# First MLP pass fed from SBUF instead of DRAM, in a three-stage transformer kernel

## The chip, the cores and the metric

The kernel runs on one NeuronCore of a Trainium2 chip. The metric is device time in microseconds (us) from one launch; three runs of the kernel before the change took 1973.47, 1975.07 and 1977.85 us, so its median is 1975.07 us.

## The reference

The inputs are q, k, v of 8 batches, 8 heads, 576 positions and 64 columns, and weights; all is float32. Cut to what matters:

```
# 1. landmark attention per batch and head (32 landmarks = means over 18 positions)
A, Bm, C = softmax(q @ k_lm.T), softmax(q_lm @ k_lm.T), softmax(q_lm @ k.T)   # scale 1/8
Z = Bm.T / (norm_1(Bm) * norm_inf(Bm) + 1e-6); six times: Z = 2Z - Z @ Bm @ Z
x = concat_heads(A @ Z @ C @ v)                      # (8, 576, 512)
# 2. token mixing of rank 32, then an MLP
u = x + ((x.T @ U) @ V).T
x = u + relu(u @ w_ch1) @ w_ch2                      # 512 -> 2048 -> 512
# 3. Fourier mixing, norm, a second MLP
u = x + real(fft(fft(x, axis=1), axis=2))
un = (u - mean(u)) / sqrt(var(u) + 1e-6)
out = u + relu(un @ moe2_w_ch1) @ moe2_w_ch2
```

## The kernel before

Activations are kept transposed: 512 features in four blocks of 128 partitions, positions along the row. The 8 x 576 positions are cut into nine **chunks** of 512 columns, so that chunk c begins 64c columns into batch c and ends in the next batch. Each float32 matmul of the MLPs is made of three products of rounded halves (high, low), for which x, g and the weights are split: ScalarE casts the high half, VectorE or GpSimd subtracts to get the low one (`split`, lines 51 and 52).

Each MLP is done in two **passes** of half its hidden layer, four passes in all (`Mlp.stream`). A pass goes through the nine chunks; a chunk takes 16 **steps**: in eight up steps (m = 0 to 7) it makes `up(m)` = 12 matmuls of 128x512 (lines 213 to 215), ScalarE's relu (217) and VectorE's low half (218); in eight down steps, two for each output block d, 24 matmuls a block (lines 258 to 260), the addition of a residual (267) and the write `dst.put`. The first pass takes its residual from the x tiles and writes y1; the second takes x anew and y1 as residual and writes x1, from which the Fourier stage (`Mixer`, one per batch, 24 steps apart, first at step 33 of the second pass) loads U at its first step (line 689) and folds it four steps later (698). Passes three and four do the second MLP.

The order of the work is written out by hand: `Slots` hold closures by step, and each engine and each DMA queue executes its instructions in the order of the program. Nearly all DMAs are issued from SyncE's queue, those of u1 from ScalarE's.

Attention of one batch (`Batch.steps`) spans relative steps 0 to 25: landmarks 0 to 3, the kernel matrix and its inverse 5 to 19 (`newton` 14 to 19), scores 6 to 11, `values` 12, `query` 12 to 14, its norm 14 and 15, `heads` 20, `rank` 21, `mix(i)` 22 to 25. `mix` multiplies out block i of u1 (with token mixing folded in), copies it from PSUM to the tile u1T, and ScalarE's queue writes that to `u1[b]` in DRAM. Blocks 2 and 3 go to rows shifted by one, since the Fourier stage wants features 257 to 511 in reverse order behind 256: block 2 to rows 257 to 384, block 3 to rows 385 to 511 (127 partitions) and, as a one-row write, row 256. Batch 0 begins at step -32, batch b at 16(b - 2); the first pass begins at step 0. In the steps ahead of that TensorE also does six small filler matmuls a step (line 935). x of chunk 0 is loaded from u1 at step -6 and split from there on; x of a later chunk is loaded in the chunk before it, at d = 1, and split from d = 2.

The weights come as float64 and are converted on chip (`convert`: per weight tile of 128x512 four yields, with four VectorE operations at lines 96, 97, 100, 103 and one at 106, one GpSimd addition at 104, ScalarE's abs at 101, then a split). For the first pass `direct` does that while attention runs: 87 yields in all with the set-up of U and V, drawn by `some(convs, n)`, n a step. Raw tiles 0 to 13 use the buffers of g, the others two of their own. Weights of later passes are converted and staged to DRAM (`staging`), and fetched into the eight w1 and eight w2 tiles.

Of the kernel before, what the change touches and what calls it, by code (L numbers as in the profile page):

```python
# [9 lines left out]
F32 = mybir.dt.float32  # L10
# [13 lines left out]
P = 128  # L24
# [15 lines left out]
def body(ctx: ExitStack, tc: tile.TileContext, qT, kT, vn, mU, mV, w11, w12, w21, w22,  # L40
# [91 lines left out]
    class ByBatch:  # L132
# [9 lines left out]
        def put(self, c, d, sb):  # L142
            for cc, b, cb in pieces(c):
                nc.sync.dma_start(self.tiles[b][rows(d), cb], sb[:, cc])

    class ByChunk:
        def __init__(self, tiles):
# [16 lines left out]
    class Mlp:  # L164
# [4 lines left out]
        def __init__(self, pool, ps, banks, passes):  # L169
            self.pool, self.ps, self.banks, self.passes = pool, ps, banks, passes  # L170
            self.w1, self.w2 = [], []
            self.n = 0

# [26 lines left out]

        def start(self):
            self.nx = []
            self.xf = self.load(0, self.passes[0][0])
            self.more = self.split_x(self.xf, nc.vector)

# [16 lines left out]
        def stream(self, p, tail=None):  # L222
            x_src, res_src, dst, _ = self.passes[p]
            for c in range(NCH):
                x, self.nx = self.nx, []
                last = c + 1 == NCH
                res = self.xf if res_src == "x" else self.tiles() if res_src is None else None
                after = (p, c + 1) if not last else (p + 1, 0) if p + 1 < len(self.passes) else None
                g = []
                for m in range(HM):  # L230
                    g.append(self.up(m, x))
                    if m == 1 and res is None:
                        res = self.load(c, res_src)
                        if tail:
                            sc = self.tail_pool.tile([P, NC], F32, name="sc", bufs=2)
                            tail[0].get(c, sc)
                            skip = [self.tail_pool.tile([P, NC], F32, name="skip", bufs=8) for _ in range(4)]
                            for d in range(4):
                                tail[1].get(c, d, skip[d])
                    if m == 3 and after and p:  # L240
                        self.xf = self.load(after[1], self.passes[after[0]][0])
                    yield 1
                if last:
                    self.w1 = self.w1[HM:]
                    if after:
                        for m in range(HM):
                            self.fetch("w1", self.passes[p + 1][3][m])
                more, w2 = iter(()), self.w2[:HM]
                for d in range(4):
                    if d == 1 and after and p == 0:  # L250
                        self.xf = self.load(after[1], self.passes[after[0]][0])
                    if d == (0 if p else 2) and after:
                        more = self.split_x(self.xf)
                    ps = self.bank()
                    for k in range(HM):
                        gh, gl = g[k][:, 0, :], g[k][:, 1, :]
                        wh, wl = w2[k][:, 0, rows(d)], w2[k][:, 1, rows(d)]
                        nc.tensor.matmul(ps, wh, gh, start=k == 0, stop=False)  # L258
                        nc.tensor.matmul(ps, wl, gh, start=False, stop=False)  # L259
                        nc.tensor.matmul(ps, wh, gl, start=False, stop=k == HM - 1)  # L260
                        if k == HM // 2 - 1:
                            next(more, 0)
                            yield 1
                    if res_src is None:
                        nc.scalar.copy(res[d], ps)
                    else:
                        nc.vector.tensor_tensor(res[d], ps, res[d], op=ALU.add)  # L267
                    if tail:
                        nc.vector.tensor_tensor(res[d], res[d], sc, op=ALU.mult)
                        nc.vector.tensor_tensor(res[d], res[d], skip[d], op=ALU.add)  # L270
                    dst.put(c, d, res[d])
                    next(more, 0)
                    yield 1
                if last:
                    self.w2 = self.w2[HM:]
                    if after:
                        for k in range(HM):
                            self.fetch("w2", self.passes[p + 1][3][HM + k])

# [10 lines left out]
    def attention_constants(cp, t):  # L290
# [8 lines left out]
        t["at"] = cp.tile([P, 4, S], F32, name="at")  # L299
        t["Bf"] = cp.tile([P, 2, P], F32, name="Bf")  # L300
        t["W"] = cp.tile([P, 4, P], F32, name="W")
        nc.gpsimd.memset(t["Bf"], 0.0)
        nc.gpsimd.memset(t["W"], 0.0)
# [23 lines left out]
    class Batch:  # L327
# [7 lines left out]

        def __init__(self, pool, psb, t, b):
            self.pool, self.psb, self.t, self.b = pool, psb, t, b
            self.E, self.ET, self.ps = {}, {}, {}
# [31 lines left out]
        def kernel(self):  # L370

            t, qb, kb = self.t, self.t["qb"], self.t["kb"]
            ps = self.bank("b")
            for g in range(2):
                for e in range(2):
# [14 lines left out]
            for e in range(2):  # L390
                sl = self.EJ[e]
                nc.vector.tensor_tensor(t["Bf"][sl, :, sl], sB[sl], r[sl].unsqueeze(2).to_broadcast([64, 2, 64]),
                                        op=ALU.mult)
            nc.vector.tensor_tensor(self.sums[:, :, 0], s, r, op=ALU.mult)

        def kernel_t(self):
            ps = self.bank("b")
            for g in range(2):
                nc.tensor.transpose(ps[:, g * P:g * P + P], self.t["Bf"][:, g, :], ident_sb)
            v = ps[:, 0:2 * P].rearrange("p (g c) -> p g c", g=2)  # L400
# [178 lines left out]
        def heads(self):  # L579
# [3 lines left out]
            for g in range(2):  # L583
                nc.tensor.matmul(ps[:, 64 * g:64 * g + 64], self.t["Bf"][:, g, :], self.ry[:, g, P:192], start=True,
                                 stop=True)
# [21 lines left out]
        def mix(self, i):  # L607
            W_, at, u = self.t["W"], self.t["at"], u1[self.b]
            u1T = self.pool.tile([P, S], F32, name="u1T", bufs=2)
            pss = []  # L610
# [5 lines left out]
            nc.scalar.copy(u1T[:, HS:S], pss[1][:, 0:HS])  # L616
            if i < 2:
                nc.scalar.dma_start(u[i * P:(i + 1) * P, :], u1T)
            elif i == 2:
                nc.scalar.dma_start(u[257:385, :], u1T)  # L620
            else:
                nc.scalar.dma_start(u[385:512, :], u1T[0:127])
                nc.scalar.dma_start(u[256:257, :], u1T[127:128])

        def steps(self, after):
# [10 lines left out]
            yield from ((14 + i, lambda i=i: self.newton(i)) for i in range(6))  # L636
            yield from ((20, self.heads), (21, self.rank))
            yield from ((22 + i, lambda i=i: self.mix(i)) for i in range(4))
            if after:
# [221 lines left out]
    class Slots:  # L861
# [9 lines left out]
        def run(self, s):  # L871
            for step in self.at.pop(s, ()):
# [6 lines left out]
            [w21[i] for i in range(HM, NM)] + [w22[i] for i in range(HM, NM)]]  # L879
    U1, X1, U2, UN, Y = ByBatch(u1), ByBatch(x1), ByBatch(u2), ByBatch(un), ByBatch([out[b] for b in range(B)])  # L880
    passes = [(U1, "x", ByChunk(y1), None), (U1, ByChunk(y1), X1, staged[1]),
              (UN, None, ByChunk(y2), staged[2]), (UN, ByChunk(y2), Y, staged[3])]
# [5 lines left out]
    with pool("mm") as mp, pool("pm", space=PSUM) as pm:  # L888
        mlp = Mlp(mp, pm, 3, passes)

        def direct():
# [20 lines left out]
            for i in range(len(ws)):  # L912
                fetch()
                new = convert(cv0, raws[i], ws[i], 2)
# [5 lines left out]

        EARLY = 14
        with pool("aa") as ap_, pool("ac") as ac, pool("cv0") as cv0, pool("pt", space=PSUM) as psb:
            t = {}
            batches = [Batch(ap_, psb, t, b) for b in range(B)]
            slots = Slots()
            FIRST = -32
            X0 = FIRST + Batch.LAST + 1
            for b in range(B):
                slots.add(FIRST if b == 0 else STEPS * (b - 2), batches[b].steps(batches[b + 1] if b + 1 < B else None))

# [6 lines left out]
            with tc.manual_schedule():  # L937
# [6 lines left out]
                for s in range(FIRST, 0):  # L944
                    slots.run(s)
                    if s > FIRST + 5:
                        filler()
                    if s == X0:
                        mlp.start()
                    elif X0 + 2 < s:  # L950
                        some(mlp.more, 2)
                    some(convs, 0 if s < FIRST + 4 else 3 if s < FIRST + 10 or s > X0 else 2)
                later, gen = staging(cv0, 1, 2), mlp.stream(0)
                for s in range(N):
                    next(gen)
                    slots.run(s)
                    if s < HM:
                        some(convs, 3)
                        if s == HM - 1:
                            some(convs, 99)  # L960
                    else:
                        some(later, 2 if s % 4 == 0 else 1)
                some(later, 999)
# [102 lines left out]
```

## Time and profile before

| | |
|---|---|
| median of three runs | 1975.07 us |
| span of the profiled execution | 1966.8 us |
| TensorE busy | 1898.4 us, 97% |
| VectorE busy | 939.6 us, 48% |
| ScalarE busy | 558.1 us, 28% |
| GpSimd busy | 366.8 us, 19% |
| DMA, read and written | 132 GB/s over the span |

Busy time counts an engine's instructions, from the first to the last of the program. The span is that of one execution taken by the hardware profiler; the profile gives its span and not a time with the launch. In the page and the views, PE is TensorE, DVE is VectorE, ACT is ScalarE, POOL is GpSimd and SP is SyncE, whose rows are DMA issues; a q behind an engine's name marks its sequencer. L213 is line 213 of the kernel.

### The profile page before, as it was taken

To read this page: it belongs to the slowest core of one execution; us is meant where nothing else is said; L and a number is where in the kernel's file an instruction comes from. 1 tells how busy PE (TensorE), PEld (TensorE's weight loads), DVE (VectorE), ACT (ScalarE), POOL (GpSimd) and SP (SyncE) were. 2 spreads that over 40 slices of the span, in tenths; PEclk is the share of its full clock that TensorE was granted. 3 is DMA by queue.
4 is the path that set the end of the run, shared out by engine and by line. 5 is a ranking of instruction groups with operands and counts; after the bars stand their busy time and mean duration, and the time that the engine had idled before them with its cause. 6 is when DMAs were issued, how large, how long until landed. Compare 5 with 4: busy or idle time off the path is not lost.

```text
span 1966.8 us, 27786 instructions
## 1 busy us (share of the span) xinstructions
PE 1898.4 (97%) x11096; PEld 1562.5 (79%) x11096; DVE 939.6 (48%) x1628; ACT 558.1 (28%) x1153; POOL 366.8 (19%) x346
## 2 busy tenths in 40 slices
PE   6778999999999999999999999999999999999998
PEld 5666777777778888888888888888888888888887
DVE  6785465555433244474574454654532133333333
ACT  2433333333322222233232333433322211111110
POOL 2441011111111122131331122313211000010000
PEclk9999999999999999999999999999999999999999
DMA  7234335343324643354453562433422453323332
GB/s 251 92 107 130 119 107 177 102 139 126 110 88 145 228 153 131 127 166 160 133 162 105 210 225 81 164 125 120 140 91 91 149 203 122 99 91 97 97 97 75
DMA packets 145874, 262.35 MB, mean 133 GB/s; under 512 B 22768, under 2 KB 77904, under 8 KB 145744
## 3 DMA queue, kind: packets, MB, share of 16 engines
q1 hardware_dynamic: 141248, 251.14, 38.2%
q10 hardware_dynamic: 4496, 9.44, 1.3%
q8 instruction: 87, 1.43, 0.3%
q14 instruction: 43, 0.35, 0.1%
HBM read 166.93 MB, written 93.59 MB: 132 GB/s over the span
## 4 chain that ended last, share of the span: by engine, by line
PE 80%; DVE 8%; DMA 6%; ACT 2%; issue 2%; ACTq 0%; POOL 0%; SPq 0%; DVEq 0%; POOLq 0%
PE ps L213 12%; PE ps L215 12%; PE ps L214 12%; PE ps L258 11%; PE ps L260 11%; PE ps L259 11%; DMA u<-u1T 5%; PE ps_f L76 1%; PE ps_f L77 1%; PE ps_f L78 1%; PE ps_n L613 1%; PE ps_n L572 1%; DVE g L218 1%; DMA xf<-u 1%; DVE cva L106 1%
## 5 line engine op out<-in xcount | busy, mean ns | idle before, releaser
L213 PE MATMUL ps<-x,w 128*128 128x512 f32 x1152 | 460.2, 399 | 1.7 <-ACT x L51 1.7
L258 PE MATMUL ps<-g,w 128*128 128x512 f32 x1152 | 458.4, 398 | 0.0
L215 PE MATMUL ps<-x,w 128*128 128x512 f32 x1152 | 450.1, 391 | 0.9 <-POOL x L52 0.9
L260 PE MATMUL ps<-g,w 128*128 128x512 f32 x1152 | 449.7, 390 | 0.0
L214 PE MATMUL ps<-x,w 128*128 128x512 f32 x1152 | 449.2, 390 | 0.0
L259 PE MATMUL ps<-g,w 128*128 128x512 f32 x1152 | 448.8, 390 | 0.0
L218 DVE SCALAR_TENSOR_TENSOR g<-ps,g 128x512 fp32r<-128x512 f32 x288 | 198.5, 690 | 459.9 <-ACT g L217 459.4
L217 ACT ACTIVATE g<-ps 128x512 fp32r<-128x512 f32 x288 | 171.9, 597 | 644.8 <-PE ps L215 644.3
L213 PEld LDWEIGHTS ps<-x,w 128*128 128x128 f32 x1152 | 216.7, 188 | 48.1 <-issue 2.8
L215 PEld LDWEIGHTS ps<-x,w 128*128 128x128 f32 x1152 | 216.3, 188 | 48.1 <-POOL x L52 1.4
L260 PEld LDWEIGHTS ps<-g,w 128*128 128x128 f32 x1152 | 216.2, 188 | 46.4
L258 PEld LDWEIGHTS ps<-g,w 128*128 128x128 f32 x1152 | 216.3, 188 | 46.2 <-issue 2.6
L259 PEld LDWEIGHTS ps<-g,w 128*128 128x128 f32 x1152 | 216.6, 188 | 43.0
L214 PEld LDWEIGHTS ps<-x,w 128*128 128x128 f32 x1152 | 216.8, 188 | 42.7
L267 DVE TENSOR_TENSOR xf<-ps,xf 128x512 f32<-128x512 f32 x108 | 74.4, 689 | 259.7 <-PE ps L260 232.1
L104 POOL TENSOR_TENSOR cvp<-cvp,cva 128x512 f32<-128x512 f32 x64 | 86.0, 1344 | 536.2 <-DVE cvp L103 536.1
L52 POOL TENSOR_TENSOR x<-xf,x 128x512 fp32r<-128x512 f32 x70 | 94.0, 1349 | 473.2 <-ACT x L51 445.1
L51 ACT CAST x<-xf 128x512 fp32r<-128x512 f32 x144 | 85.3, 618 | 60.4 <-DMA xf<-u 60.1
L52 POOL TENSOR_TENSOR stg<-cva,stg 128x512 fp32r<-128x512 f32 x48 | 68.7, 1431 | 133.7 <-ACT stg L51 133.7
L52 DVE TENSOR_TENSOR x<-xf,x 128x512 fp32r<-128x512 f32 x74 | 53.8, 729 | 69.4 <-ACT x L51 68.6
L101 ACT ACTIVATE wraw<-wraw 128x512 f32<-128x512 f32 x50 | 34.1, 682 | 134.3 <-DVE cva L97 134.3
L572 PE MATMUL ps_n<-ry 128*128 128x192 f32 (+1 forms) x192 | 40.3, 334 | 23.2 <-DVE ry L576 23.2
(279 smaller groups left out, 1812.1 us busy)
## 6 DMA issues: line engine op xcount, KB each, us to landing
wraw<-w SPq DMA_DIRECT2D x50, 512.0 KB
d<-stg SPq DMA_DIRECT2D x48, 512.0 KB
w<-d SPq DMA_DIRECT2D x48, 512.0 KB
y<-xf SPq DMA_DIRECT2D x72, 256.0 KB
xf<-y SPq DMA_DIRECT2D x72, 256.0 KB
U<-x SPq DMA_DIRECT2D x8, 1152.0 KB
u<-U SPq DMA_DIRECT2D x8, 1152.0 KB
un<-Z SPq DMA_DIRECT2D x16, 576.0 KB
```

The lines of the kernel that those rows point to most:

```text
L51: nc.scalar.copy(hi, src)
L52: (eng or nc.vector).tensor_tensor(lo, src, f32(hi), op=ALU.subtract)
L104: nc.gpsimd.tensor_tensor(pf, pf, af, op=ALU.add)
L213: nc.tensor.matmul(ps, wh, xh, start=k == 0, stop=False)
L214: nc.tensor.matmul(ps, wl, xh, start=False, stop=False)
L215: nc.tensor.matmul(ps, wh, xl, start=False, stop=k == 3)
L217: nc.scalar.activation(g[:, 0, :], ps, AF.Relu)
L218: nc.vector.scalar_tensor_tensor(out=g[:, 1, :], in0=ps, scalar=0.0, in1=f32(g[:, 0, :]), op0=ALU.max, op1=ALU.subtract)
L258: nc.tensor.matmul(ps, wh, gh, start=k == 0, stop=False)
L259: nc.tensor.matmul(ps, wl, gh, start=False, stop=False)
L260: nc.tensor.matmul(ps, wh, gl, start=False, stop=k == HM - 1)
L267: nc.vector.tensor_tensor(res[d], ps, res[d], op=ALU.add)
```

## The change

The diff, cut to its core:

```
+    class ForFolds(ByBatch):                       # dst of the second pass (x1) now
+        def put(self, c, d, sb):
+            for cc, b, cb in pieces(c):
+                x = self.tiles[b]
+                if d < 2:
+                    nc.sync.dma_start(x[rows(d), cb], sb[:, cc])
+                elif d == 2:
+                    nc.sync.dma_start(x[257:385, cb], sb[:, cc])
+                else:
+                    nc.sync.dma_start(x[385:512, cb], sb[0:127, cc])
+                    nc.sync.dma_start(x[256:257, cb], sb[127:128, cc])
...
-        def start(self):                           # loaded x of chunk 0
+        def get_tail(self, c):
+            self.xt = self.tiles()
+            for k in range(4):
+                nc.sync.dma_start(self.xt[k][:, 0:64 * c], u1[c - 1][rows(k), S - 64 * c:S])
+        def hand_tail(self, c, k):
+            t = self.pool.tile([P, 2, NC], F32R, name="x", bufs=4)
+            self.nx.append(t)
+            n = 64 * c
+            if n:
+                split(t[:, 0, 0:n], t[:, 1, 0:n], self.xt[k][:, 0:n], nc.gpsimd if k % 2 else nc.vector)
+        def hand_head(self, c, k, u1T):
+            n = 64 * c
+            t = self.nx[k]
+            split(t[:, 0, n:NC], t[:, 1, n:NC], u1T[:, 0:NC - n], nc.gpsimd if k % 2 and c > 1 else nc.vector)
... stream
-                res = self.xf if res_src == "x" else self.tiles() if res_src is None else None
+                res = self.tiles() if res_src is None else None
-                    if m == 3 and after and p:
+                    if m == 3 and after and (p or last):
                         self.xf = self.load(after[1], self.passes[after[0]][0])
-                    if d == 1 and after and p == 0:
-                        self.xf = self.load(after[1], self.passes[after[0]][0])
-                    if d == (0 if p else 2) and after:
+                    if d == 0 and after and (p or last):
                         more = self.split_x(self.xf)
-                        wh, wl = w2[k][:, 0, rows(d)], w2[k][:, 1, rows(d)]
+                        w = w2[2 * d + k // 4]
+                        wh, wl = w[:, 0, rows(k % 4)], w[:, 1, rows(k % 4)]
                     dst.put(c, d, res[d])
                     next(more, 0)
+                    if last and after:
+                        for k in range(2 * d, 2 * d + 2):
+                            self.fetch("w2", self.passes[p + 1][3][HM + k])
-                    if after:                      # behind the four blocks
-                        for k in range(HM):
-                            self.fetch("w2", self.passes[p + 1][3][HM + k])
... Batch.mix
+            if self.b == 0:
+                self.mlp.hand_tail(0, i)
-            if i < 2:
-                nc.scalar.dma_start(u[i * P:(i + 1) * P, :], u1T)
-            elif i == 2:
-                nc.scalar.dma_start(u[257:385, :], u1T)
-            else:
-                nc.scalar.dma_start(u[385:512, :], u1T[0:127])
-                nc.scalar.dma_start(u[256:257, :], u1T[127:128])
+            nc.scalar.dma_start(u[rows(i), :], u1T)
+            self.mlp.hand_head(self.b, i, u1T)
... Batch.steps
+            if self.b:
+                yield 18, lambda: self.mlp.get_tail(self.b)
+                yield from ((20 + k // 2, lambda k=k: self.mlp.hand_tail(self.b, k)) for k in range(4))
...
-    passes = [(U1, "x", ByChunk(y1), None), (U1, ByChunk(y1), X1, staged[1]),
+    passes = [(U1, U1, ByChunk(y1), None), (U1, ByChunk(y1), X1, staged[1]),
... direct
-                fetch()
+                if len(raws) < EARLY or len(raws) < i + 2:
+                    fetch()
-        EARLY = 14
+        EARLY = 8
-            FIRST = -32
-            X0 = FIRST + Batch.LAST + 1
+            FIRST = -1 - Batch.LAST                # -26
-                slots.add(FIRST if b == 0 else STEPS * (b - 2), ...)
+                slots.add(STEPS * (b - 1) - 12 if b else FIRST, ...)
+            slots.add(STEPS * (B - 1) + 6, [(0, lambda: mlp.get_tail(B))])
+            slots.add(STEPS * (B - 1) + 8, ((k, lambda k=k: mlp.hand_tail(B, k)) for k in range(4)))
-                    some(convs, 0 if s < FIRST + 4 else 3 if s < FIRST + 10 or s > X0 else 2)
+                    some(convs, 0 if s < FIRST + 4 else 2)
-                    if s < HM:
-                        some(convs, 3)
-                        if s == HM - 1:
+                    if s < STEPS:
+                        some(convs, 4)
+                        if s == STEPS - 3:
                             some(convs, 99)
                     else:
-                        some(later, 2 if s % 4 == 0 else 1)
+                        some(later, 2 if s % 2 == 0 else 1)
```

So `mix` splits its block of u1 from u1T straight into the x tiles of the chunk that begins in this batch, and only a chunk's first 64c columns are read back from DRAM; batch 0 ends at step -1 and the stream follows at step 0. u1 stays in the plain order of rows, and the shift by one row moves to the write of x1. Each w2 tile holds all that half an output block needs, not one hidden block for all four. Beside this, the block matrix Bf gets two copies, used by even and odd batches, and the host lays out the weights' columns to match.

## Rows read from the trace of the kernel before

**Rows 1.** The page: busy time of TensorE; TensorE's busy tenths in 40 slices.
```profile
PE 1898.4 (97%) x11096; PEld 1562.5 (79%) x11096; DVE 939.6 (48%) x1628; ACT 558.1 (28%) x1153; POOL 366.8 (19%) x346
...
PE   6778999999999999999999999999999999999998
```

**Rows 2.** Busy time by stretch: stretch, length, five engines' busy us, TensorE's clock, DMA.
```profile
0.00:83.40 83.40, 59.82 (x664) 50.93 (x665) 61.91 (x140) 29.11 (x74) 26.75 (x42) 0.94 0.52 184
83.40:113.20 29.80, 18.17 (x307) 16.80 (x306) 24.08 (x41) 10.59 (x22) 10.94 (x9) 0.83 0.58 205
113.20:152.20 39.00, 33.47 (x235) 25.47 (x234) 32.74 (x55) 15.43 (x35) 18.65 (x20) 1.00 0.10 33
152.20:193.20 41.00, 35.48 (x355) 27.52 (x354) 20.69 (x47) 12.07 (x29) 7.20 (x6) 0.94 0.38 116
262.10:329.80 67.70, 65.29 (x588) 51.94 (x586) 37.64 (x82) 22.92 (x56) 10.00 (x15) 1.00 0.41 136
529.70:583.80 54.10, 54.10 (x321) 44.38 (x320) 20.00 (x36) 15.71 (x34) 6.10 (x5) 1.00 0.25 85
631.00:674.60 43.60, 43.60 (x194) 36.09 (x194) 12.34 (x19) 8.34 (x14) 5.88 (x6) 1.00 0.66 211
```

**Rows 3.** TensorE in order of time, 58 to 116 us: start, us, what, idle before.
```profile
80.67 1.14 PE L613 MATMUL ps_n<-at,W 128*128 128x288 f32 x4
...
92.00 0.67 PE L482 MATMUL ps_b<-v__594,ET 128*32 128x64 f32 x32 [4.64 <-ACT ETt L468]
...
109.63 1.65 PE L572 MATMUL ps_n<-ry 128*128 128x192 f32 x4 [6.99 <-DVE ry L576]
...
113.25 0.48 PE L213 MATMUL ps<-x,w 128*128 128x512 f32 x1
```

**Rows 4.** ScalarE in order of time, the same stretch.
```profile
84.59 4.92 ACTq L623 DMA_DIRECT2D u<-u1T  x1
...
104.12 1.14 ACT L51 CAST x<-xf 128x512 fp32r<-128x512 f32 x2
```

**Rows 5.** All instructions of line 623: durations in ns, min/median/max.
```profile
L623 ACTq DMA_DIRECT2D u<-u1T x8: 919/7632/8857, 84.6 to 568.4; - x8
```

**Rows 6.** VectorE by line, 113.2 to 193.2 us: busy us, mean ns, idle before.
```profile
L97 DVE SCALAR_TENSOR_TENSOR cva<-g,cva 128x512 uint32<-128x512 uint32 x3 | 4.0, 1337 | 0.1
...
L106 DVE SCALAR_TENSOR_TENSOR cva<-g,cvp 128x512 f32<-128x512 f32 x4 | 2.8, 692 | 0.0
...
L100 DVE TENSOR_SCALAR cvp<-cva 128x512 uint32<-128x512 uint32 x6 | 2.6, 426 | 0.1
...
L103 DVE SCALAR_TENSOR_TENSOR cvp<-g,cvp 128x512 f32<-128x512 uint32 x3 | 2.1, 692 | 0.1
```

**Rows 7.** Waits of SyncE's queue: total us, times, longest.
```profile
SPq L140 <- DMA u<-u1T: 120.0, 8, 16.7
```

**Rows 8.** Waits of TensorE, 113 to 675 us.
```profile
PE ps_n L572 <- DVE ry L576: 11.7, 7, 3.3
PE ps_b L482 <- ACT ETt L468: 3.8, 4, 1.2
```

**Rows 9.** The chain that ended last, pieces in order of time: start, us, what.
```profile
235.82 17.93 DMA u<-u1T
254.19 3.06 DMA xf<-u
```

**Rows 10.** TensorE by line and form, 296 to 330 us.
```profile
L503 PE MATMUL ps_c<-kb,q__2645 128*32 128x64 f32 x128 | 2.2, 220 | 0.0
L572 PE MATMUL ps_n<-ry 128*128 128x192 f32 x8 | 1.7, 339 | 1.2 <-DVE ry L576 1.2
L482 PE MATMUL ps_b<-v__2614,ET 128*32 128x64 f32 x64 | 1.3, 222 | 1.2 <-ACT ETt L468 1.2
```

**Rows 11.** SyncE and VectorE in order of time, 757 to 786 us.
```profile
766.73 0.43 SPq L689 DMA_DIRECT2D U<-x  x1
...
779.62 2.00 DVE L698 TENSOR_TENSOR big<-U 128x1152 f32<-128x1152 f32 x1
```

More of the change, by code (lines that the diff above doesn't have):

```diff
@@ L171, in __init__ @@
             self.w1, self.w2 = [], []
-            self.n = 0
+            self.nx = []
         def bank(self):
@@ L199, in split_x @@
                 yield 1
-        def start(self):
-            self.nx = []
-            self.xf = self.load(0, self.passes[0][0])
-            self.more = self.split_x(self.xf, nc.vector)
+        def get_tail(self, c):
[12 more added lines that the diff above has]
+            split(t[:, 0, n:NC], t[:, 1, n:NC], u1T[:, 0:NC - n], nc.gpsimd if k % 2 and c > 1 else nc.vector)
         def up(self, m, x):
@@ L299, in attention_constants @@
         t["at"] = cp.tile([P, 4, S], F32, name="at")
-        t["Bf"] = cp.tile([P, 2, P], F32, name="Bf")
+        t["Bf0"], t["Bf1"] = (cp.tile([P, 2, P], F32, name=f"Bf{n}") for n in range(2))
         t["W"] = cp.tile([P, 4, P], F32, name="W")
-        nc.gpsimd.memset(t["Bf"], 0.0)
+        nc.gpsimd.memset(t["Bf0"], 0.0)
+        nc.gpsimd.memset(t["Bf1"], 0.0)
         nc.gpsimd.memset(t["W"], 0.0)
@@ L334, in body, with __init__ @@
         QUARTERS = [slice(32 * h, 32 * h + 32) for h in range(4)]
-        def __init__(self, pool, psb, t, b):
-            self.pool, self.psb, self.t, self.b = pool, psb, t, b
+        def __init__(self, pool, psb, t, b, mlp):
+            self.pool, self.psb, self.t, self.b, self.mlp = pool, psb, t, b, mlp
             self.E, self.ET, self.ps = {}, {}, {}
@@ L373 @@
             ps = self.bank("b")
+            self.Bf = t[f"Bf{self.b % 2}"]
             for g in range(2):
@@ L391 @@
                 sl = self.EJ[e]
-                nc.vector.tensor_tensor(t["Bf"][sl, :, sl], sB[sl], r[sl].unsqueeze(2).to_broadcast([64, 2, 64]),
+                nc.vector.tensor_tensor(self.Bf[sl, :, sl], sB[sl], r[sl].unsqueeze(2).to_broadcast([64, 2, 64]),
                                         op=ALU.mult)
@@ L398, in kernel_t @@
             for g in range(2):
-                nc.tensor.transpose(ps[:, g * P:g * P + P], self.t["Bf"][:, g, :], ident_sb)
+                nc.tensor.transpose(ps[:, g * P:g * P + P], self.Bf[:, g, :], ident_sb)
             v = ps[:, 0:2 * P].rearrange("p (g c) -> p g c", g=2)
@@ L583, in heads @@
             for g in range(2):
-                nc.tensor.matmul(ps[:, 64 * g:64 * g + 64], self.t["Bf"][:, g, :], self.ry[:, g, P:192], start=True,
+                nc.tensor.matmul(ps[:, 64 * g:64 * g + 64], self.Bf[:, g, :], self.ry[:, g, P:192], start=True,
                                  stop=True)
@@ L879, in body @@
             [w21[i] for i in range(HM, NM)] + [w22[i] for i in range(HM, NM)]]
-    U1, X1, U2, UN, Y = ByBatch(u1), ByBatch(x1), ByBatch(u2), ByBatch(un), ByBatch([out[b] for b in range(B)])
-    passes = [(U1, "x", ByChunk(y1), None), (U1, ByChunk(y1), X1, staged[1]),
+    U1, X1, U2, UN, Y = ByBatch(u1), ForFolds(x1), ByBatch(u2), ByBatch(un), ByBatch([out[b] for b in range(B)])
+    passes = [(U1, U1, ByChunk(y1), None), (U1, ByChunk(y1), X1, staged[1]),
               (UN, None, ByChunk(y2), staged[2]), (UN, ByChunk(y2), Y, staged[3])]
@@ L919, in direct @@
             yield from old
-        EARLY = 14
+        EARLY = 8
         with pool("aa") as ap_, pool("ac") as ac, pool("cv0") as cv0, pool("pt", space=PSUM) as psb:
             t = {}
-            batches = [Batch(ap_, psb, t, b) for b in range(B)]
+            batches = [Batch(ap_, psb, t, b, mlp) for b in range(B)]
             slots = Slots()
-            FIRST = -32
-            X0 = FIRST + Batch.LAST + 1
+            FIRST = -1 - Batch.LAST
             for b in range(B):
-                slots.add(FIRST if b == 0 else STEPS * (b - 2), batches[b].steps(batches[b + 1] if b + 1 < B else None))
+                slots.add(STEPS * (b - 1) - 12 if b else FIRST, batches[b].steps(batches[b + 1] if b + 1 < B else None))
+            slots.add(STEPS * (B - 1) + 6, [(0, lambda: mlp.get_tail(B))])
+            slots.add(STEPS * (B - 1) + 8, ((k, lambda k=k: mlp.hand_tail(B, k)) for k in range(4)))
             def filler():
@@ L947, in body @@
                         filler()
[L948 to L951, printed above, removed]
-                    some(convs, 0 if s < FIRST + 4 else 3 if s < FIRST + 10 or s > X0 else 2)
+                    some(convs, 0 if s < FIRST + 4 else 2)
                 later, gen = staging(cv0, 1, 2), mlp.stream(0)
@@ L1037, in pairs, with w1, w2 @@
         return np.ascontiguousarray(a).reshape(B, P, 4, S)
-    def w1(a):
-        a = a[order].reshape(4, P, FF // P, P).transpose(2, 1, 0, 3)
+    def w1(a, o):
+        a = a[o].reshape(4, P, FF // P, P).transpose(2, 1, 0, 3)
         return np.ascontiguousarray(a).reshape(FF // P, P, DM).view(np.uint64)
-    def w2(a):
-        return np.ascontiguousarray(a[:, order].reshape(FF // P, P, DM)).view(np.uint64)
+    def w2(a, o):
+        a = a[:, o].reshape(2, 2, 4, P, 4, P).transpose(0, 4, 1, 3, 2, 5)
+        return np.ascontiguousarray(a).reshape(FF // P, P, DM).view(np.uint64)
     arrays = {
@@ L1050 @@
         "mV": np.ascontiguousarray(inputs["moe_V"]).view(np.uint64),
-        "w11": w1(inputs["moe_w_ch1"]), "w12": w2(inputs["moe_w_ch2"]),
-        "w21": w1(inputs["moe2_w_ch1"]), "w22": w2(inputs["moe2_w_ch2"]),
+        "w11": w1(inputs["moe_w_ch1"], cols), "w12": w2(inputs["moe_w_ch2"], cols),
+        "w21": w1(inputs["moe2_w_ch1"], order), "w22": w2(inputs["moe2_w_ch2"], order),
         **_tables(),
```

## The prediction

> **What bounds the kernel now.** I read the page first. TensorE is busy for 97% of the span, and only the first slices of its row stand below 9 [rows 1]: what can be won lies ahead of the first MLP matmul, or in work that TensorE needn't do. So the second view is busy time by stretch, cut where the trace shows the first up matmul (113.2 us) and the chunk boundaries of the first pass [rows 2]. One chunk without attention takes 43.6 us (631.0 to 674.6); a chunk that carries one batch's attention 67.7, of which TensorE is idle 2.4; the first chunk takes 39.0 + 41.0 = 80.0. Ahead of it lie 113.2 us with 59.8 + 18.2 = 78 of TensorE.
>
> The third view is TensorE in order of time between the last attention product and the first up matmul [rows 3]. Batch 0's last `mix` ends at 80.67 + 1.14 = 81.8; the stream begins at 113.25. In these 31.4 us TensorE waits 4.64 (on ScalarE's copy ETt) and 6.99 (on a VectorE sum), and for the rest runs batch 1 and filler. ScalarE shows why the stream can't begin sooner [rows 4]: issuing the one-row write of the last u1T piece holds it from 84.59 for 4.92 us, and the last two casts of x, loaded back from DRAM, come at 104.12. The eight such issues take 0.9 to 8.9 us, median 7.6 [rows 5]. The last number is VectorE's: busy 32.7 of 39.0 us in the first up phase. There it is nearly the bound, since it carries attention, the low halves of g and the conversion of the weights.
>
> From 674.6 us on the only edits are the last rows of the x1 write, the order of the w2 fetches and the w2 columns. Time here is the trace's; its span is 1966.8 us, the median of the runs 1975.07, so 8.3 us lie outside the span, and I carry them over unchanged.
>
> **The change, part by part.**
>
> *The prologue, 113.2 us.* It goes from 32 to 26 steps, and the last `mix` of batch 0 moves from the 26th step of 32 to the last. What ran up to 81.8 us stays ahead of the stream, with two more steps of batch 1 (transposes, about 1 us of TensorE) and without 6 of 50 conversion units (a weight has four). Behind the last mix come two copies of u1T, one cast and one subtract on 448 to 512 columns, about 2.1 us at the durations of the trace's own splits (0.56 a cast in [rows 4], 0.69 a VectorE operation in [rows 6]); three of the four k have their tile earlier, so up(0) can begin on them. The round trip through DRAM and the one-row issue are gone. I take 85. Bounds: 82 (nothing late) and 95 (batch 1's stages pile up as they do before 92.0 us now). Against 113.2 this is 28 less, but not all of it is a gain: what stood there has to go somewhere.
>
> *Work that moves out.* Batch 1 now has 12 of its steps ahead of the stream, not 16, and each later batch keeps that lag of 4. Chunks 0 to 5 hold a whole batch each as before; the four steps turn up in chunk 6. They are values, query and two Newton products, 1.3 + 2.2 + 1.7 = 5.2 us in one chunk [rows 10], 6 with the smaller forms. Chunk 6: 54.1 [rows 2] + 6 = 60.
>
> *Chunk 0, 80.0 us.* Conversion now runs at 2 units a step ahead of the stream and 4 in it. Of 87 units 45 are done when it begins (68 before), so 42 are left, 10.5 weights where 4.75 were. The eight up steps convert 8. One weight costs VectorE 1.34 (line 97, which is 0.69 when nothing disturbs it) + 0.69 + 0.69 + 2 x 0.43 = 3.6 us [rows 6]; 3.25 more in the up phase are 11.7. They also hold steps 12 to 15 of batch 1 (softmax of the queries) instead of later, lighter ones, about 3 us more. 32.7 + 11.7 + 3 = 47.4 us of VectorE; at the share it reached here (0.84) the phase lasts 56. The down phase keeps its 41.0 less the waits for x and u1T at both ends, about 8 with its steps 8 to 15 that leave it: 33. Chunk 0: 89. Bounds: 80 (VectorE's extra work fits, as if it hid behind TensorE) and 102: raw weights from the ninth on now have two buffers and are fetched one ahead, each fetch waiting until the weight before last is converted, so VectorE may wait on each of eight; an estimate of 1.5 us each, the load of 1 MB of x having taken 3.06 [rows 9] plus its issue, in a step of about 7 us. Behind that wait in VectorE's order stand the low halves of g, and TensorE waits for those. I lie near the middle, as [rows 2] show VectorE at 84% under the lighter load.
>
> *Chunks 1 to 5, 336.5 us.* Here a chain of the write of u1, 17.93 us, the load of x, 3.06, and a split ends on the next chunk's first matmul [rows 9]. SyncE waits 120 us in 8 times for that write [rows 7]. x now comes from SBUF three steps before its chunk, and only the first columns by way of DRAM, written a chunk earlier. But TensorE's idle time is not 17.9 a chunk: it is 2.4 in 67.7, and from the first up matmul on it is 11.7 us for Newton sums and 3.8 for ETt in all [rows 8]. Newton's six products now all lie in up steps, where VectorE also has g to serve, so I return half: 331.5. Bounds: 327 (all idle goes) and 338. Each split becomes two pieces for k of a chunk; ScalarE is below 40% busy there, so they cost nothing (if that cover went, four casts of 0.56, 2 us a chunk). The residual is loaded at the second step of a chunk and needed after the tenth; its load moves on SyncE ahead of conversion fetches and hides.
>
> *Chunks 7 and 8, 90.8 us.* x for chunk 7 no longer waits: 88. *Sum:* 85 + 89 + 331.5 + 60 + 88 = 653.5 against 674.6: 21 less.
>
> *The second pass.* The rows of x1 are permuted when it is written: at the end of each chunk one write has 127 partitions, twice where a chunk spans two batches (seven of nine), each followed by a one-row write, on SyncE's queue. Of such a write [rows 9] show 17.9 us. Queued behind are the staging store, the residual, the mixer's U and the next x. U is issued at 766.73, and VectorE takes it at 779.62 without a wait [rows 11]; a landing 10 us later would hold VectorE 6 us and TensorE some 3, as the low halves of g for the first down block stand behind it. Three mixers load right behind a chunk's end. I take 3 us for all; bounds 0 and 16. The permutation of the weights' columns and the w2 order cost nothing: the matmuls are the same in number and shape, and fetches that start up to six steps sooner are covered by a down phase of 21.8 us (half of 43.6). The second Bf is one memset of POOL at the start, behind loads.
>
> 21 - 3 = 18: 1975 - 18 = **1957 us**.
>
> [...]
>
> **The rivals.**
>
> *The prologue's gain is kept whole* (chunk 0 at 80 as before, prologue 82, chunks 1 to 5 without idle): 9 + 3 + 4.5 = 16 us less than forecast, **1941**. For it: POOL and ScalarE have room in chunk 0, and TensorE's own work there is only 69 us. Against: VectorE at 84%.
>
> *VectorE and the raw loads eat it* (prologue 90, chunk 0 at 102): 18 more than forecast, **1975**, no change. For it: one raw tile ahead, and residual, v, q and raws all want SyncE in steps 1 to 3. Against: DMA is busy only a tenth of the first up phase [rows 2].
>
> *The second pass stalls: slower.* If a pair of 127-row writes takes 2 x 17.9 = 36 us in order and the loads behind it wait, the residual lands after about 40 us, while it is wanted after an up phase and one down block: 21.8 + 5.4 = 27, and 32 with a mixer's work. 8 us in each of seven chunks is 56: **2013**. It decides once a pair takes more than some 28 us. Against: the 17.9 were under load, on pieces of full length; two pieces together move no more bytes than one did.
>
> **How the numbers follow.** Forecast 0.53; gain kept whole 0.20; eaten 0.17; slower by the second pass 0.10. Its own range is 1946 to 1968. The range for eight in ten is 1938 to 1978: it leaves out the third rival and the best end of the first. A measurement of this kernel can tell 0.2%, 4 us. The forecast and the first rival count as faster; the second, which ends on the old time, is spread as 0.03 faster, 0.09 same and 0.05 slower; the third is slower. That gives 0.76, 0.09 and 0.15.
>
> **What would show it.** The first up matmul at 82 to 95 us instead of 113.25; no idle ScalarE behind line 623's issue; the first up phase longer than 39 us with VectorE near 0.85; chunks 1 to 4 nearer to 66 than 67.6, chunk 6 near 60; the first pass ending near 653. In the second pass SyncE's issues behind each chunk's last write late, with VectorE's line 698 waiting for U at three mixers. It is wrong if the stream still begins after 100, if chunk 0 exceeds 105, or if TensorE idles by more than 3 us at chunk ends of the second pass.

## The result, and the profile after

The changed kernel takes 1953.25 us (median of 4 runs, 1953.05 to 1953.68), the kernel before 1975.38 beside it: a ratio of 0.9893, interval 0.9879 to 0.9907, 22 us less. Forecast were 1957, 18 less, in a range from 1938 to 1978.

By its stretches the first pass went almost as forecast. The view of busy time by stretch of the changed kernel, cut as in [rows 2]: prologue, first up and first down phase, chunks 1 to 5 together, chunk 6, chunk 7, and of the second pass the chunk in which the mixers begin; columns as there.

```profile
0.00:83.10 83.10, 62.14 (x674) 52.49 (x675) 60.53 (x138) 30.89 (x77) 23.84 (x40) 0.94 0.49 176
83.10:127.50 44.40, 35.49 (x421) 28.27 (x420) 35.92 (x66) 17.66 (x36) 20.55 (x18) 0.96 0.41 131
127.50:172.20 44.70, 36.88 (x168) 26.70 (x168) 29.38 (x65) 16.18 (x43) 14.69 (x16) 0.92 0.32 107
172.20:503.50 331.30, 327.13 (x2924) 259.53 (x2921) 193.13 (x426) 122.35 (x304) 59.70 (x84) 1.00 0.43 145
503.50:563.70 60.20, 60.18 (x544) 48.81 (x543) 24.98 (x52) 20.56 (x46) 8.34 (x9) 1.00 0.36 122
563.70:607.20 43.50, 43.50 (x193) 36.05 (x192) 16.65 (x24) 9.32 (x16) 8.36 (x8) 1.00 0.38 132
737.80:791.70 53.90, 51.75 (x242) 42.14 (x240) 24.91 (x37) 13.99 (x29) 14.60 (x10) 0.97 0.37 120
```

The stream begins at 83.1 us, as TensorE in order of time shows, answering to [rows 3]: the last `mix`, filler, and the first up matmul without a gap.

```profile
80.23 1.14 PE L644 MATMUL ps_n<-at,W 128*128 128x288 f32 x4
...
81.86 1.50 PE L966 MATMUL ps<-ident_sb 128*128 128x128 f32 x12
83.11 0.48 PE L241 MATMUL ps<-x,w 128*128 128x512 f32 x1
```

The first pass ends at 650.8 instead of 674.6. In the second pass VectorE waits for the mixer's U at three mixers; its waits from 690 to 1400 us:

```profile
DVE big L727 <- DMA U<-x: 10.2, 3, 5.5
```

The three chunks concerned grow from 49.6, 51.7 and 51.4 to 53.9, 53.5 and 54.0 us, 8.7 together. The third and fourth passes last 441.5 and 397.0 us, as before. The two profiled executions differ by 15.3 us (1966.8 and 1951.5), the runs by 22: the one taken of the kernel before was shorter than its median.

### The profile page after: what moved, and what is told of

Its sections match the earlier page's. It is cut to its first block, busy times and chain, and to the rows that moved or that the text cites. A ratio compares the mean times of both kernels' runs of the same rounds, so it can differ in the third digit from the quotient of the medians.

```text
span 1951.5 us, 27671 instructions
## 1 busy us (share of the span) xinstructions
PE 1894.6 (97%) x11024; PEld 1554.2 (80%) x11024; DVE 936.0 (48%) x1644; ACT 564.6 (29%) x1181; POOL 373.2 (19%) x359
## 4 chain that ended last, share of the span: by engine, by line
PE 86%; DVE 8%; DMA 3%; ACT 2%; issue 1%; SPq 0%; ACTq 0%; POOL 0%; DVEq 0%
PE ps L285 13%; PE ps L287 13%; PE ps L286 13%; PE ps L241 12%; PE ps L243 12%; PE ps L242 11%; DMA U<-x 1%; PE ps_f L76 1%; PE ps_f L77 1%; PE ps_f L78 1%; PE ps_n L644 1%; PE ps_n L601 1%; PE ps L966 1%; DVE g L246 1%; DVE cva L106 1%
## 5 line engine op out<-in xcount | busy, mean ns | idle before, releaser
L241 PEld LDWEIGHTS ps<-x,w 128*128 128x128 f32 x1152 | 216.7, 188 | 43.5
L52 POOL TENSOR_TENSOR x<-xf,x 128x512 fp32r<-128x512 f32 (+7 forms) x70 | 85.9, 1234 | 525.8 <-ACT x L51 491.7
L51 ACT CAST x<-xf 128x512 fp32r<-128x512 f32 (+7 forms) x140 | 75.1, 575 | 0.4
L106 DVE SCALAR_TENSOR_TENSOR cva<-wraw,cvp 128x512 f32<-128x512 f32 x56 | 50.2, 897 | 29.7 <-POOL cvp L104 29.7
L52 DVE TENSOR_TENSOR x<-xf,x 128x512 fp32r<-128x512 f32 (+7 forms) x70 | 50.1, 715 | 29.9 <-ACT x L51 28.5
```

The costliest lines, as they stand in the source:

```text
L51: nc.scalar.copy(hi, src)
L52: (eng or nc.vector).tensor_tensor(lo, src, f32(hi), op=ALU.subtract)
L241: nc.tensor.matmul(ps, wh, xh, start=k == 0, stop=False)
```

## The experiments

**The kernel before again.** No edit.

> The kernel before, unchanged. Its profiled span was 1966.8 us against a median of 1975 in the timed runs, while the changed kernel has 1951.5 against 1953.25. If that profiled execution was simply one of the shorter ones, this run's span is 1970 to 1974 and the times stay at 1975. If 8 us really lie outside the span of this kernel, the span is 1966 to 1968 again.

Measured 1973.93 us; its profiled run took 1971.36 with a span of 1969.5. About 2 us lie outside a span, not 8. The span itself is just under the range expected for a shorter execution, 1970 to 1974. The kernel before spreads from 1969.8 to 1978 in 19 runs, at a mean granted clock of 0.993 to 0.987; the changed one stayed within 0.6 us in its 4. Chunk 7 shows a part of it: TensorE is idle for 2 to 3 us of it in both executions, waiting for x, but it lasts 47.2 us in one and 49.5 in the other, where the mean granted clock over the chunk was 0.93 instead of 1.00. First the trace before, then this run:

```profile
583.80:631.00 47.20, 44.62 (x193) 35.82 (x193) 15.69 (x25) 11.08 (x19) 10.17 (x8) 1.00 0.38 126
```
```profile
584.30:633.80 49.50, 47.42 (x193) 37.62 (x192) 15.69 (x25) 11.09 (x19) 10.17 (x8) 0.93 0.37 121
```

The rest of the 8 us is not traced: the two spans differ by 2.7 us, most of it here.

**Even rows for u1, nothing else.** The rival that the prediction did not have: the change gains by the shape of one write.

```
 # kernel before, Batch.mix, i == 3
-nc.scalar.dma_start(u[385:512, :], u1T[0:127])
+nc.scalar.dma_start(u[385:497, :], u1T[0:112])
+nc.scalar.dma_start(u[497:512, :], u1T[112:127])
```

> The kernel before, with only the 127-row write of u1 cut into 112 and 15 rows on the same queue. My theory (most of the gain is the shorter prologue and x taken from SBUF): ScalarE's holds of 7.6 us and the late x at chunk ends go, which is worth TensorE's 10 us of idle time in chunks 1 to 7 and some 5 to 8 us ahead of the stream; 1958 to 1966. Rival (the change gains by the write's shape alone): 1953 or less.

Measured 1948.28 us (ratio 0.9869, 0.9849 to 0.9890): 5 us better than the whole change. The prologue, chunk 0 and chunks 1 to 5 of this kernel (chunk 6 takes 54.1 us, as in [rows 2]):

```profile
0.00:112.80 112.80, 82.40 (x971) 71.52 (x971) 88.10 (x181) 40.07 (x94) 38.39 (x50) 0.88 0.55 194
112.80:188.70 75.90, 68.30 (x587) 52.34 (x586) 51.54 (x101) 27.52 (x64) 24.77 (x25) 0.98 0.25 82
188.70:513.20 324.50, 324.50 (x2921) 259.69 (x2920) 183.88 (x406) 116.34 (x280) 48.65 (x71) 1.00 0.39 131
```

The prologue is as long as before, so its length was not the write's doing. But chunks 1 to 5 take 324.5 instead of 336.5, with TensorE busy throughout; the first pass ends at 654.4, 20.2 sooner. My theory expected 1958 or more and is refuted: the write's shape alone brings more than the whole change, and that rival came true.

**The odd write put back into the changed kernel.**

```
 # changed kernel, Batch.mix
-nc.scalar.dma_start(u[rows(i), :], u1T)
+if i < 3:
+    nc.scalar.dma_start(u[rows(i), :], u1T)
+else:
+    nc.scalar.dma_start(u[384:511, :], u1T[0:127])
+    nc.scalar.dma_start(u[511:512, :], u1T[127:128])
```

> The changed kernel, with the last block of u1 written as 127 rows and one row again, as before the change, in plain order. My theory: x no longer depends on that write, but ScalarE is held again for some 7 us in each of eight batches, on the scores of the next one; 0.5 to 2 us a chunk, 1957 to 1968. Rival (the order of the steps hides it): 1952 to 1955.

Measured 1974.04 us, the old time (ratio 0.9998, 0.9988 to 1.0007). The first pass ends at 669.8. Both expectations missed, mine by 6 us. The hold of ScalarE, the time in which it does nothing but issue the one-row write [rows 5], now stands ahead of the cast of x for the next chunk, for 5.31 us at the end of the prologue. The first up matmuls show it, here and then in the changed kernel; behind the last bar is TensorE's idle time before them:

```profile
L241 PE MATMUL ps<-x,w 128*128 128x512 f32 x1152 | 461.6, 401 | 12.1 <-ACT x L51 12.1
```
```profile
L241 PE MATMUL ps<-x,w 128*128 128x512 f32 x1152 | 460.4, 400 | 0.0
```

Chunks 1 to 6, which took 331.3 + 60.2 = 391.5 us in the changed kernel, take 399.1 here, chunk 0 takes 96.3 instead of 89.1, and chunk 7 49.5 instead of 43.5, with one wait of 4.0 us for that cast.

So there are four corners, by the end of the first pass:

| | 127 + 1 rows | even rows |
|---|---|---|
| order of before | 674.6 (677.3 in the repeat) | 654.4 |
| changed order | 669.8 | 650.8 |

The write's shape is worth 20 and 19 us, the new order with x from SBUF 5 and 4. Each corner is one execution, and the two with 127 + 1 rows spread: with the repeat the 20 becomes 23 and the 5 becomes 7.5. The medians of the runs show the same order: 1973.8 against 1948.3 us for the write alone, and 1948.3 against 1944.8 for the new order with every write even (below).

**Which half of the odd write costs: the hold or the late landing?** The one-row write is issued first, so nothing stands behind the long one on ScalarE's queue.

```
 # kernel before, Batch.mix, i == 3
+nc.scalar.dma_start(u[256:257, :], u1T[127:128])
 nc.scalar.dma_start(u[385:512, :], u1T[0:127])
-nc.scalar.dma_start(u[256:257, :], u1T[127:128])
```

> The kernel before, with the one-row write of u1 issued ahead of the 127-row write, so that nothing stands behind the long one on ScalarE's queue; it still lands late. If the cost of the odd shape is ScalarE's hold (median 7.6 us a batch): as with the even rows, 1948 to 1955. If it is the late landing (x of the next chunk 18 us late, split at the chunk's end): 1968 to 1975.

Measured 1949.47 us (0.9876, 0.9859 to 0.9894). Two swapped lines gain more than the change. Line 623, now the long write, is issued at once, where [rows 5] had a median of 7632 ns; SyncE waits for u1's landing as long as in [rows 7]. The issues of the line (shortest, median and longest in ns, first and last start in us), then SyncE's waits (sum, count, longest):

```profile
L623 ACTq DMA_DIRECT2D u<-u1T x8: 232/272/288, 85.0 to 550.6; - x8
```
```profile
SPq L140 <- DMA u<-u1T: 115.9, 13, 14.5
```

So ScalarE's hold was the cost. The late landing alone cost little: the first pass ends at 655.6 us against 654.4 with even rows, with chunk 7 at 46.1 us against 43.5. One row names what the hold kept back, the copy of the transposed scores from 60 to 600 us. First the kernel before, then this one; behind the last bar is ScalarE's idle time before it:

```profile
L461 ACT COPY ET<-ps_c 128x512 f32<-128x512 f32 x14 | 7.7, 587 | 54.4 <-issue 41.2 <-PE ps_b L466 7.4 <-PE ps_c L459 5.9
```
```profile
L461 ACT COPY ET<-ps_c 128x512 f32<-128x512 f32 x14 | 8.2, 587 | 36.7 <-PE ps_c L459 36.7
```

"issue" is the profile's word for waiting for nothing that it shows: these 41.2 us, in five batches, are the hold. Not all of it was lost, since without it the same copy waits 36.7 us for TensorE: ScalarE's idle time there falls by 17.7. What in the queue makes the issue take so long no run shows.

**Even rows for x1 in the changed kernel.**

```
 # ForFolds.put, last block
-nc.sync.dma_start(x[385:512, cb], sb[0:127, cc])
+nc.sync.dma_start(x[385:497, cb], sb[0:112, cc])
+nc.sync.dma_start(x[497:512, cb], sb[112:127, cc])
```

> The changed kernel, with the 127-row write of x1 in the second pass cut into 112 and 15 rows; the one-row write stays. [...] Rival (the issue of the one-row write holds SyncE and all behind it): nothing changes, 1952 to 1954.

Measured 1944.75 us (0.9853, 0.9836 to 0.9871), 8.5 better than the change and under the 1952 to 1954 of the rival. The chunk with the first mixer is back to the length it had:

```profile
736.90:786.50 49.60, 49.60 (x242) 41.25 (x240) 25.32 (x37) 14.00 (x29) 14.55 (x10) 1.00 0.40 130
```

The other two last 51.7 and 51.4, and VectorE's waits for U are gone. The issue of the one-row write falls from a median of 3.5 us to 0.25, and SyncE's waits for x1's landing go too, so this run alone doesn't say which of the two made U late. In the chunk shown, U is issued 13.8 us behind the chunk's start in the changed kernel, 3.9 of it a wait of SyncE for x1's landing, and 6.4 us behind it here: both have a part.

**The same swap on SyncE's queue.** In the changed kernel the one-row writes of x1 go first.

```
 # ForFolds.put, last block
+nc.sync.dma_start(x[256:257, cb], sb[127:128, cc])          # for each piece
+...
 nc.sync.dma_start(x[385:512, cb], sb[0:127, cc])            # then for each piece
-nc.sync.dma_start(x[256:257, cb], sb[127:128, cc])
```

> The changed kernel, with the one-row writes of x1 issued ahead of the 127-row ones. In the kernel before, the same swap for u1 on ScalarE's queue brought the whole gain. On SyncE's queue something always follows: the staging store, the residual, U. If the long write holds whatever DMA comes next, or delays its landing, VectorE still waits some 10 us for U in all and the time stays at 1951 to 1954. [...]

Measured 1956.67 us (0.9914, 0.9898 to 0.9931): no better than the changed kernel, rather 3 us worse, above the range expected. U is still late, as VectorE's waits show, and SyncE in order of time behind the chunk's last block (the long writes are line 160):

```profile
DVE big L729 <- DMA U<-x: 11.7, 3, 5.4
```
```profile
739.75 1.09 SPq L160 DMA_DIRECT2D x<-xf  x2
740.94 4.54 SPq L118 DMA_DIRECT2D d<-stg  x1
```

The hold has moved to what stands behind the pair of long writes, the staging store of 128 rows, which takes 4.54 us to issue where its line has a median of 0.32. On ScalarE's queue nothing followed for the rest of the batch.

**What bounds chunk 0.** The conversion of the eight w2 tiles is left out.

```
 # direct()
-new = convert(cv0, raws[i], ws[i], 2)
+new = convert(cv0, raws[i], ws[i], 2) if i < HM else bare(raws[i], ws[i])   # bare: split only
```

> The changed kernel, leaving out the conversion arithmetic of the eight w2 tiles of the first pass (they are only split, from the high words). Theory: chunk 0 lasts 89 us because VectorE has to convert in it; 8 x 2.9 us less work of VectorE brings it to 70 to 76 and the time to 1936 to 1941. Rival (chunk 0 is held by the latency from product to product of two batches' attention): 84 to 89 and 1948 to 1954.

Measured 1933.91 us (0.9799, 0.9773 to 0.9826), a little under the range expected. Chunk 0 takes 69.9 us, also just under:

```profile
82.40:120.20 37.80, 34.68 (x422) 28.29 (x420) 27.23 (x47) 16.44 (x34) 14.96 (x17) 0.95 0.47 150
120.20:152.30 32.10, 32.10 (x168) 24.87 (x168) 15.96 (x43) 13.41 (x38) 7.36 (x9) 1.00 0.49 153
```

VectorE loses 22 us of work and chunk 0 19 us: conversion sets its length, in both halves. That it is VectorE's share of the conversion is likely, not shown: GpSimd loses 13 us and ScalarE 4 as well.

**Where to convert.** Three splits of the same work between prologue and chunk 0, all with even x1 rows.

```
 # ahead of the stream, units a step; (in the stream)
 some(convs, 0 if s < FIRST + 4 else 2)                                # changed kernel (4)
-some(convs, 0 if s < FIRST + 4 else 3 if s >= FIRST + 10 else 2)      # rates3 (3)
-some(convs, 0 if s < FIRST + 4 else 2 if s < FIRST + 18 else 1)       # less (4)
-some(convs, 0 if s < FIRST + 4 else 2 if s < FIRST + 14 else 1)       # least (4)
```

> The changed kernel with even x1 rows, and conversion at 3 units a step from the eleventh step on and 3 in the stream (2 and 4 there). If VectorE is full throughout, work only moves: the stream begins at 88 to 91, chunk 0 takes 79 to 83, 1943 to 1947. Rival (VectorE idles 22 of 83 us ahead of the stream and takes it for nothing): the stream begins by 85, 1936 to 1941.

> The changed kernel with even x1 rows (1944.75), and the last 8 steps ahead of the stream converting at 1 unit a step, not 2. In the run with 3 units a step, 18 units more there cost 18 us and gave back 8 in chunk 0. If that slope holds downwards, 8 units less give the stream a start 6 to 8 us earlier (75 to 77) and chunk 0 4 us more (93): 1940 to 1943. Rival (2 units a step fit behind attention, only 3 were too many): the start stays at 80 to 82 and chunk 0 grows: 1946 to 1950.

> As the kernel with 1 unit in the last 8 steps, with 1 unit from the fifteenth step on (12 units less than with 2). The w2 tiles are then ready in the very step in which they are wanted. By the same slope: the start at 72 to 74, chunk 0 at 95: 1938 to 1942. Rival (without a step of slack each output block waits for its weights' split): chunk 0 at 100 or more, 1946 to 1952.

| | start of stream | chunk 0 | time, us (ratio) |
|---|---|---|---|
| 3 units | 100.4 | 81.1 | 1955.42 (0.9889 to 0.9931) |
| 2 units | 82.4 | 88.9 | 1944.75 (0.9836 to 0.9871) |
| 1 in the last 8 | 75.6 | 94.1 | 1942.08 (0.9828 to 0.9860) |
| 1 in the last 12 | 71.8 | 99.9 | 1944.82 (0.9837 to 0.9875) |

The expectation for 3 units, that work only moves, was wrong, and so was its rival: from 3 units to 2 the stream begins 18.0 us sooner and chunk 0 grows by 7.8, so these 16 units (not 18, as the next expectation says) cost ahead of the stream twice what they cost inside; the rate in the stream changed with them, from 3 to 4. The advantage shrinks from there: the next step returns 6.8 for 5.2, near what was expected, the last 3.8 for 5.8, between its expectation and the rival. The prologue at 3 units and at 1 in the last eight:

```profile
0.00:100.40 100.40, 66.15 (x674) 56.33 (x675) 74.70 (x155) 34.19 (x83) 33.49 (x47) 0.88 0.42 149
```
```profile
0.00:75.60 75.60, 56.84 (x674) 48.29 (x675) 52.89 (x129) 28.70 (x74) 19.26 (x37) 1.00 0.54 192
```

VectorE is busy for 74 and 70% of it, so neither is full. TensorE is busy for 66% of the longer one, at a mean granted clock of 0.88, and for 75% of the shorter, at 1.00. Why a unit costs more ahead of the stream is not shown beyond that. With 1 unit in the last 8 steps the kernel is the fastest of those that do all of the work, 11 us below the changed one; the 2.7 between it and 2 units are little, though its longest run (1943.1) is under the shortest of the other (1943.9).

**The hand-over itself.** Chunk 0 takes x by way of DRAM again.

```
 # changed kernel; mix no longer hands over batch 0
+mlp.xf = mlp.load(0, U1)
+for _ in mlp.split_x(mlp.xf, nc.vector):
+    pass
```

> The changed kernel, with chunk 0 alone taking x from DRAM again: written, loaded and split behind the last mix. Theory: the first up matmul comes some 10 us later, and chunk 0 gives back about half of it, since VectorE converts meanwhile: 1956 to 1960. Rival (the round trip hides behind what VectorE has to do anyway): 1953 to 1955. If nothing is given back: 1963 or more.

Measured 1958.32 us (0.9902 to 0.9941), 5 us more. The stream starts at 83.6, not 10 us later, since each block goes by itself: the loads of two are issued before the last `mix` ends at 80.3, the last at 82.8, and TensorE waits 1.3 us for a cast of x. Chunk 0 takes 92.2 instead of 89.1. The time lies in the range of the theory, but not for its reason. The round trip that [rows 3] and [rows 4] seemed to show, 31 us, is worth some 4 (5 by the runs) once the write is even: what filled it was the order of the steps, as the even write in the old order still has 112.8 us ahead of the stream.

## Why the prediction was right, and where its reasons were not

The time fell inside the range and near the forecast, in part by luck. Term by term, forecast against trace: prologue 85 and 83.1; chunk 0 89 and 89.1; chunks 1 to 5 331.5 and 331.3; chunk 6 60 and 60.2; chunks 7 and 8 88 and 87.1; the second pass plus 3 and plus 8.7. Behind these sums the following steps don't hold.

*The step that failed in its reason* is that for chunks 1 to 5: "TensorE's idle time is not 17.9 a chunk: it is 2.4 in 67.7 ... so I return half". The even write alone returns 12 us there, all of the waits (9.9 us there: 6.1 for Newton sums, 3.8 for ETt) and what they slow behind them, 4 in chunk 0, 4 in chunk 7. The new order gives 6.8 of the 12 back (331.3 against 324.5). That a return of 5 came out is two errors that cancel. The row that told it was read and not priced: a median of 7.6 us for issuing one row [rows 5]. I charged it by the 3.8 us in which TensorE waits for ETt by name [rows 8]. It holds ScalarE, and with it x, scores and Newton sums, whose waits stand under other names: those for Newton sums, which I laid to VectorE, go with the even write too.

*The prologue was priced right and credited wrongly.* "28 less, but not all of it is a gain": with the even write as the base, it is 29.7 less ahead of the stream, and 13.2 come back in chunk 0, 6.8 in chunks 1 to 5, 6.1 in chunk 6. That leaves 3.6. No rival of the prediction had the write's shape do it alone, and that is what the runs showed.

*Chunk 0's halves.* 56 and 33 were forecast, 44.4 and 44.7 came. VectorE was busy 35.9 us in the up phase, not 47.4: line 97 ran at 0.69 us all ten times, not the 1.34 of [rows 6], and six conversions passed that line there, where eight were counted; four did in the down phase. VectorE waited 0.2 us for raw loads, for which the upper bound had 1.5 each; that estimate also took the 3.06 us of [rows 9] for 1 MB of x, while the row is one of the eight loads that bring it. TensorE waits 8.9 us in the up phase, 6.3 of it for Newton sums, and 7.8 in the down phase, 3.3 of it for u1T. That the misses of the two halves cancel to 0.1 us is luck; that the sum is near has a reason, as conversion lengthens both.

*The second pass* went by the mechanism named: U behind the 127-row writes, three mixers, TensorE's low halves behind it. Its term was sized at 3 and is 8.7: in the first of the three chunks 2.2 of 4.3 us are idle time of TensorE, and the rest is longer busy time at a mean granted clock of 0.97. Why the write's shape costs this no run shows, only the times: u1's write of 127 rows took 17.93 us to land [rows 9], the 15 rows of the even write, issued behind its 112, 5.8 in the median (3.8 to 6.5). So cut, x1's write costs 8.5 us less, and u1's 20 us less in the first pass. The third rival, with 56 us, did not come: VectorE never waits for the residual in that pass. That a pair of long writes takes 36 us in order was a supposition, and no run shows it; SyncE's longest wait for x1's landing is 4.7 us.

*The base.* "8.3 us lie outside the span" is wrong; 2 us do. The profiled execution of the kernel before was at the short end of its spread (with 2 us, 1968.8; the shortest timed run of that kernel took 1969.5), so a sum on the trace had to miss some 7 us of gain. The first pass gained 3 us more than forecast, and the second pass's extra loss of 5.7 hid most of both. This is the luck in the forecast's 1957.

## What to carry to other kernels

Price an issue that takes microseconds on a compute engine's queue by all that stands behind it on that engine, not by the wait that bears its name elsewhere; "issue" as the end of a wait is the mark to look for. A write of 127 rows can be cut into pieces, here 112 and 15 (1948.3 us where the kernel before takes 1974), or issued last on a queue where nothing follows (1949.5). When several parts of a change touch one stretch, undo each alone: here a sum that was right to 0.2% had the gain in the wrong part.

## What the runs showed of the hardware

A one-row DMA behind a 127-row DMA on the same queue held the issuing engine for up to 8.9 us on ScalarE's queue [rows 5] and 7.1 on SyncE's, in the changed kernel; behind 112 and 15 rows its issue took at most 0.29 us on ScalarE's queue and 0.25 in the median on SyncE's. Issued ahead of the long one it took 0.24 us in the median on either, and on SyncE's queue the DMA behind the long ones was held instead, though it has 128 rows (4.54 us behind a pair). A chunk in which TensorE is idle for 2 to 3 us took 47.2 us at a mean granted clock of 1.00 in one execution, and 49.5 at 0.93 in another of the same kernel.
